# Where to form two small weight sums: GpSimd in the first GEMM of block 1, or VectorE in its second GEMM

## Chip, core and metric

The kernel runs on one core of one Trainium2 chip. The metric is the time of one execution on the device in microseconds. The engines named below are PE (TensorE; its weight loads are listed apart as PEld), DVE (VectorE), ACT (ScalarE), POOL (GpSimd) and SP (SyncE, which here only issues transfers).

## What is computed

A retention layer feeds a feed-forward block. All data are fp32.

```python
# retention, per batch and head: gamma_h = 1 - 2**(-5-h), scale = 1/sqrt(64)
state = gamma * state + outer(k[t], v[t])
y[t]  = scale * q[t] @ state
x = y.transpose(0, 2, 1, 3).reshape(3072, 512)      # 4 batches x 768 tokens, 8 heads x 64
# feed-forward
h = x @ w_in                                        # 512 -> 2048, the first GEMM
g = where(h > 0, h, exp(min(h, 0)) - 1)             # ELU
out = g @ w_out                                     # 2048 -> 512, the second GEMM
```

## The kernel before

The 3072 tokens are cut into six blocks of 512, called 0 to 5. Both GEMMs save products in the manner of Strassen: a product of two matrices, each cut in 2x2 quarters, is made of seven smaller products M1 to M7 of sums of quarters, and the results are put together from their sums. Block 0 has a plain first GEMM and Strassen once in the second. Block 1 has Strassen once in the first GEMM and twice (a Strassen inside each of the seven products) in the second. Blocks 2 to 5 have it twice in the second GEMM, and in the first for two of the seven products, M2 and M3.

The Strassen inside M2 and M3 of the first GEMM needs four sums of quarters of their weights, for each of the two. These eight "small" sums are the subject here. They are the same for all blocks, so they are made once, sent to DRAM (`scratch3`) and fetched again in each of blocks 2 to 5 through a ring of 11 weight tiles (`wq`, pool `ring`), which `fetch_small` fills: each product that has used a tile asks for the next fetch. The fetches, the loads of new tokens and the stores all go through SP's one queue, in the order of the program.

The order on every engine is the order in which the program writes the instructions (`manual_schedule`). Generators are used to interleave: `first(n)` is one of four steps (n = 0 to 3) of block 1's first GEMM, `second_twice(1, ...)` its second GEMM, and each `yield` is a place where other work can be put.

The parts that matter here, with their lines in the kernel before:

- `first(n)` (L728) goes through `strassen` (L698). Product 7 starts a new accumulation in the single PSUM bank `pd`. The same bank was last read by `plus(pd, u2)` (L695) for product 4 of the step before. So the first weight load of product 7 waits for that VectorE addition. In step n the products are written as 1, 2, then the rest of the step before (3, 4, and the ELU of its last quarter), then 6, 7, 5. The ELU of a quarter is two ScalarE operations (L477, L478) and one VectorE operation (L481).
- `sides[n]` are VectorE sums for later steps, put between the products of step n: `combine_w_in` (L674) and the remaining part of `combine_w_out` (L647), whose results are sent by `send_small` (L641).
- `combine_small(j)` (L810) makes the four small sums of M2 (j = 2) or M3 (j = 3) on GpSimd, in a tile `wi` of the pool `stage`. It is called at the end of step n = 0 for M2 and of step n = 2 for M3, followed by `send_small`.
- `scale_v(m)` (L275, L281) multiplies the v of a loaded chunk of 128 tokens by a table; from chunk 2 on it runs on GpSimd. `load(8)` to `load(11)` are written one in each step n, and the four `scale_v(8)` to `scale_v(11)` after the loop, behind `combine_small` on GpSimd.
- The pools `stage` and `t4` are then closed (L1302), and `ring` and `tpool` take their memory.
- `second_twice(1, ...)` (L933): for each of seven outer products in the order 1, 2, 6, 7, 5, 3, 4, `inner(j)` (L967) runs seven inner products of four 128x128 matmuls. PE sees them as 1, 2, then 3 and 4 of the outer product before, then 6, 7, 5. Inner product 4 adds to the PSUM bank `pd` after VectorE has read it in `add(res[:, 1, 1], pd, ...)` (L983), so its first weight load waits for that addition. `input_parts` (L941) makes four VectorE sums (`ts`, L827) for the next outer product.
- The loop at L1318 counts outer products in `step` and puts the retention of block 2 (`retention_step`) at the places in `VISITS`. `outputs_step` starts with two small copies (`seen`, L378) that wait for PE.
- `xt_` (L266) holds the activations x of block 1. They are read last by the first GEMM of block 1. The memory is written again in block 2 by `combine_x_parts` (L454).

Of the kernel before, what the change touches and what calls it, by code (L numbers as in the profile page):

```python
# [9 lines left out]
FP32 = mybir.dt.float32  # L10
# [8 lines left out]
def kernel(  # L19
# [32 lines left out]
    nc = tc.nc  # L52
    PSUM = bass.MemoryType.PSUM
    P = nc.NUM_PARTITIONS
# [29 lines left out]
    stage = early.enter_context(tc.tile_pool(name="stage", bufs=3))  # L84
# [14 lines left out]
    def load(m, parts=1):  # L99

        if m >= NCHUNK:
            return
        t = ldpool.tile([P, 2048], FP32, name="chunk", tag="chunk")
        raw[m] = (
            t[:, 0:1024].rearrange("p (a h c) -> p a h c", a=2, c=C),
            t[:, 1024:2048].rearrange("p (a h d) -> p a h d", a=2, d=D),
        )
        for part in range(parts):
            c = slice(part * 2048 // parts, (part + 1) * 2048 // parts)
            nc.sync.dma_start(t[:, c], qkv[m, :, c])  # L110

    def hold(t, other):

        if other is not None:
            nc.gpsimd.tensor_copy(t[0:1, 0:1], other[0:1, 0:1])
# [6 lines left out]
    w_a, w_b, w_s = ([x[:, n] for n in range(NQ)] for x in (w_a_, w_b_, w_s_))  # L122
# [100 lines left out]
    for h in range(H):  # L223
# [11 lines left out]
        out=causal, in_=causal, compare_op=ALU.is_gt, fill=1.0, base=0, pattern=[[-1, P]], channel_multiplier=1  # L235
# [30 lines left out]
    xt_ = const.tile([P, 4, 2, TH], FP32, name="xt")  # L266
# [45 lines left out]
    def scores(tb, pp):  # L312

        sc = [ps_r.tile([P, 2, HP, D], FP32, name="sc", tag="r") for _ in range(2)]
        for x in range(2):
            score_products(sc, tb, pp, x)
        for a in range(2):
            nc.vector.tensor_tensor(
                out=raw[tb * CPB + 2 * pp + a][0][:, 1].rearrange("p h c -> p (h c)").rearrange("p (n t) -> p n t", t=D),
                in0=sc[a].rearrange("p x h t -> p (x h) t"),  # L320
                in1=cmask.unsqueeze(1).to_broadcast([P, 2 * HP, D]), op=ALU.mult,
            )
# [29 lines left out]
    def states(tb, pp):  # L352

        kvs = [ps_r.tile([P, 2, HP, D], FP32, name="kv", tag="r") for _ in range(2)]
        for x in range(2):
            state_products(kvs, tb, pp, x, range(2))
        for x in range(2):
            for sub in range(2):
                state_sum(kvs, tb, pp, x, sub)
# [4 lines left out]
    def outputs(tb, pp):  # L364

        y = [ps_r.tile([P, 2 * 2, 2, D], FP32, name="y", tag="r") for _ in range(2)]
        for x in range(2):
            for j in range(4):
                pt = raw[tb * CPB + 2 * pp + j // 2][0][:, 1].rearrange("p h c -> p (h c)")
                within(tb, pp, x, j, y, lambda p: pt[:, (x * HP + p) * D :][:, 0:D])  # L370
        for other in range(2):
            if not other:
                yield
            else:

                for sub in range(2):
                    seen = epool.tile([P, 8], FP32, name="seen", tag="seen")
                    nc.vector.tensor_copy(seen.rearrange("p (j x) -> p j x", x=2), y[sub][:, :, :, 0])  # L378
                yield
            for x in range(2):  # L380
                across(tb, pp, x, other, y)
        i = chunks[tb * CPB + 2 * pp][1]
        for sub in range(2):
            nc.vector.tensor_tensor(
                out=place_of(x_of(tb)[:, :, 2 * pp * C : 2 * (pp + 1) * C])[:, :, :, sub, :], in0=y[sub],
                in1=place_of(powers[:, :, i * C : (i + 2) * C])[:, :, :, sub, :], op=ALU.mult,
            )
# [26 lines left out]
    def outputs_of_first():  # L414

        y = [bank(x).rearrange("p a (b x d) -> p (a b) x d", b=2, x=2) for x in "bd"]
        for x in range(2):
            for j in range(4):
                pt = raw[x][0][:, 1].rearrange("p h c -> p (h c)")
                within(0, 0, x, j, y, lambda p: pt[:, ((j // 2) * HP + p) * D :][:, 0:D])  # L420
            yield
            across(0, 0, x, 0, y)
            for sub in range(2):
                if not fresh(0, 2 * x + sub):
                    seen = epool.tile([P, 8], FP32, name="seen", tag="seen")
                    nc.vector.tensor_copy(seen[:, 0:4], y[sub][:, :, x, 0])
            if x:
                yield
            across(0, 0, x, 1, y)
            if x:  # L430
                yield
            for sub in range(2):
                nc.vector.tensor_tensor(
                    out=place_of(xb[:, :, 0 : 2 * C])[:, :, x, sub, :], in0=y[sub][:, :, x],
                    in1=place_of(powers[:, :, 0 : 2 * C])[:, :, x, sub, :], op=ALU.mult,
                )
            if not x:
                yield

    def outputs_step(tb, step):  # L440

        if step == 0:
            held["y"] = [outputs(tb, pp) for pp in range(2)]
        if step < 2:
            next(held["y"][step])
            next(held["y"][step])
        else:
            for g in held["y"]:
                next(g, None)
# [18 lines left out]
    def flush():  # L468
        while later:
            later.pop(0)()  # L470
# [109 lines left out]
    def small_of_pieces(at):  # L580

        sources = [
            (decoded[2 * NQ + n].rearrange("p r (d c) -> p (r d) c", d=2)[:, 1:4], sums[n])
            for n in (2 * at, 2 * at + 1)
        ]
        return combine_w_out(at, *sources)
# [54 lines left out]
    def send_small():  # L641
        while to_send:
            nc.sync.dma_start(*to_send.pop(0))
# [163 lines left out]

    W_IN = {2: w_a_[:, :, :, 1], 3: w_s_[:, :, 2]}

    def combine_small(j, behind=None):  # L810

        t = stage.tile([P, 4, 4, P], FP32, name="wi", tag="stage")
        hold(t.rearrange("p k f d -> p (k f d)"), behind)
        a11, a12, a21, a22 = (W_IN[j][:, 2 * r : 2 * r + 2, :, c, :] for r in range(2) for c in range(2))
        s1, s2, s3, s4 = (t[:, k].rearrange("p (n f) c -> p n f c", f=2) for k in range(4))
        tt = lambda o, x, y, op: nc.gpsimd.tensor_tensor(out=o, in0=x, in1=y, op=op)
        tt(s1, a21, a22, ALU.add)
        tt(s2, s1, a11, ALU.subtract)
        tt(s3, a11, a21, ALU.subtract)
        tt(s4, a12, s2, ALU.subtract)  # L820
        to_send.append((scratch3[j - 1], t.rearrange("p k f d -> p (k f d)")))

    xs = {}

# [295 lines left out]
    y = outputs_of_first()  # L1120
# [39 lines left out]
    y = outputs(0, 1)  # L1160
# [24 lines left out]
    for n, _ in enumerate(inner):  # L1185
# [19 lines left out]
        elif n == 12:  # L1205
            smalls = small_of_pieces(0)
# [12 lines left out]
    for n in second_of_first():  # L1219
# [6 lines left out]
        elif n == 1:  # L1226
            smalls = small_of_pieces(1)
# [33 lines left out]
    def retention_step(tb, step):  # L1261
        if tb >= NTB:
            return
        if step == 0:
            scores(tb, 0)
            scores(tb, 1)
        elif step == 1:
            states(tb, 0)
            states(tb, 1)
        elif step < 5:  # L1270
            outputs_step(tb, step - 2)
# [4 lines left out]
    sides = [  # L1276
        itertools.chain(combine_w_in(1), last), itertools.chain(combine_w_in(2), combine_w_in(3)), iter(()), iter(()),
    ]
    smalls = [2], [], [3], []
    for n in range(NQ):  # L1280
        load(2 * CPB + n)
        cur = first(n)
        for at in range(3):
            next(cur)

        for _ in tail:
            pass
        for s in cur:
            next(sides[n], None)
            next(sides[n], None)  # L1290
            if s == "gap":
                break
        for _ in sides[n]:
            pass
        tail = cur
        for j in smalls[n]:
            combine_small(j, w_s[1].rearrange("p s a b c -> p (s a b c)") if j == 2 else None)
        send_small()
    for m in range(2 * CPB, 3 * CPB):
        scale_v(m)  # L1300
# [14 lines left out]
        pass  # L1315
    flush()
    step, VISITS = 0, [(0, "end"), (2, "middle"), (3, "first"), (4, "end"), (5, "end")]
    for s in sec:  # L1318
        if s == "first":
            step += 1  # L1320
        at = (step, s if s in ("first", "middle") else "end")
        if at in VISITS:
            retention_step(2, VISITS.index(at))
        if s == ORDER2[-1]:
            break
    tail = sec
# [2 lines left out]
    for tb in range(2, NTB):  # L1329
        more = tb + 1 < NTB  # L1330
        qa, qd, u2, end = {}, {}, {}, None
# [43 lines left out]
        for n in range(NQ):  # L1375
# [17 lines left out]
            end = first_end(n, "C12", qa[n])  # L1393
            other = first_end(n, "C22", qa[n], m7)
            if n < 3:
# [5 lines left out]
                end = first_end(n, "C21", qd[n], u2[n])  # L1401
# [10 lines left out]
        end = first_end(3, "C21", qd[3], u2[3])  # L1412
# [64 lines left out]
```

## Time and profile before

| quantity | value |
|---|---|
| time, median of 3 runs | 636.76 us (635.6 to 637.08) |
| span of the profiled run | 634.4 us |
| PE busy | 626.7 us (99%) |
| DVE busy | 481.7 us (76%) |
| ACT busy | 252.9 us (40%) |
| POOL busy | 40.6 us (6%), 40 instructions |
| mean DMA rate | 216 GB/s |
| PE's share of the chain that ended last | 94% |

The chain that ended last is the list of work that set the end, followed back from the last instruction. Where an engine has 94% of it, only time in which that engine stands still can be won by moving other work. The rest of the reading is therefore a search for places where PE, or its weight load PEld, waits.

In this trace block 1's first GEMM lies at about 135 to 182 us and its second GEMM at about 182 to 240 us, counted from the start of the span.

### The profile page before, as it was taken

To read this page: it belongs to the slowest core of one execution; us is meant where nothing else is said; L and a number is where in the kernel's file an instruction comes from. 1 tells how busy PE (TensorE), PEld (TensorE's weight loads), DVE (VectorE), ACT (ScalarE), POOL (GpSimd) and SP (SyncE) were. 2 spreads that over 40 slices of the span, in tenths; PEclk is the share of its full clock that TensorE was granted. 3 is DMA by queue.
4 is the path that set the end of the run, shared out by engine and by line. 5 is a ranking of instruction groups with operands and counts; after the bars stand their busy time and mean duration, and the time that the engine had idled before them with its cause. 6 is when DMAs were issued, how large, how long until landed. Compare 5 with 4: busy or idle time off the path is not lost.

```text
span 634.4 us, 16149 instructions
## 1 busy us (share of the span) xinstructions
PE 626.7 (99%) x6680; PEld 560.7 (88%) x6680; DVE 481.7 (76%) x870; ACT 252.9 (40%) x472; POOL 40.6 (6%) x40
## 2 busy tenths in 40 slices
PE   8999999999999999999999999999999999999998
PEld 5764568888899999889999989999988999988997
DVE  5779979978879685589676598867489878558975
ACT  6599635014551113554112556111465311366311
POOL 1111000003600000200000100000110000000000
PEclk9999999999999999999999999999999999999999
DMA  8698867687477778504889701789820697700794
GB/s 336 264 390 307 269 205 222 189 248 258 176 239 228 242 254 272 239 2 135 277 267 312 290 4 55 258 283 286 302 100 4 218 299 236 238 24 2 231 309 158
DMA packets 75897, 136.85 MB, mean 216 GB/s; under 512 B 6320, under 2 KB 31792, under 8 KB 70704
## 3 DMA queue, kind: packets, MB, share of 16 engines
q1 hardware_dynamic: 75824, 135.82, 64.2%
q8 instruction: 53, 0.87, 0.5%
q14 instruction: 20, 0.16, 0.1%
HBM read 114.56 MB, written 21.23 MB: 214 GB/s over the span
## 4 chain that ended last, share of the span: by engine, by line
PE 94%; DVE 4%; issue 1%; ACT 0%; DVEq 0%
PE pa L953 20%; PE pa L911 10%; PE pd L953 10%; PE pb L953 5%; PE pa L865 5%; PE pb L911 4%; PE pa L521 3%; PE qa L911 3%; PE x L611 3%; PE pa L740 2%; PE pd L865 2%; PE qd L911 2%; PE pd L911 2%; PE pa L611 2%; PE y L394 2%; PE kv L338 2%
## 5 line engine op out<-in xcount | busy, mean ns | idle before, releaser
L961 ACT COPY ms<-pa 128x128 f32<-128x128 f32 x104 | 27.6, 265 | 147.1 <-PE pa L953 143.7
L953 PE MATMUL pa<-ts,wq 128*128 128x128 f32 x560 | 74.2, 275 | 0.0
L953 PE MATMUL pd<-ts,wq 128*128 128x128 f32 x552 | 73.6, 276 | 0.1
L953 PEld LDWEIGHTS pa<-ts,wq 128*128 128x128 f32 x560 | 68.5, 192 | 0.4
L953 PEld LDWEIGHTS pd<-ts,wq 128*128 128x128 f32 x552 | 67.1, 192 | 0.9 <-DVE res L965 0.5
L953 PE MATMUL pa<-gC,wq 128*128 128x128 f32 x480 | 64.6, 278 | 0.0
L478 ACT ACTIVATE r<-r 128x512 f32<-128x512 f32 x96 | 60.5, 631 | 3.0
L953 PEld LDWEIGHTS pa<-gC,wq 128*128 128x128 f32 x480 | 59.0, 192 | 1.3
L477 ACT ACTIVATE r<-gC 128x512 f32<-128x512 f32 x64 | 39.9, 624 | 32.0 <-DVE gC L919 32.0
L965 DVE TENSOR_TENSOR res<-pd,ms 128x128 f32<-128x128 f32 x68 | 19.4, 286 | 39.6 <-PE pd L953 38.4
L281 POOL TENSOR_TENSOR chunk<-chunk,vf 128x512 f32<-128x512 f32 x22 | 26.3, 1199 | 318.4 <-DMA chunk<-in_qkv_dram 153.5
L481 DVE SCALAR_TENSOR_TENSOR gC<-r,gC 128x512 f32<-128x512 f32 x64 | 44.3, 724 | 0.7 <-ACT r L478 0.7
L827 DVE TENSOR_TENSOR ts<-gC,ts 128x512 f32<-128x512 f32 x60 | 41.3, 688 | 1.0
L827 DVE TENSOR_TENSOR ts<-gC 128x512 f32<-128x512 f32 x60 | 40.9, 682 | 0.0
L953 PE MATMUL pb<-gC,wq 128*128 128x128 f32 x240 | 31.7, 275 | 0.0
L986 ACT COPY res<-pa 128x128 f32<-128x128 f32 x34 | 9.0, 265 | 55.1 <-PE pa L953 55.1
L953 PEld LDWEIGHTS pb<-gC,wq 128*128 128x128 f32 x240 | 29.2, 192 | 0.0
L690 ACT COPY m<-pa 128x512 f32<-128x512 f32 x24 | 13.9, 581 | 30.1 <-PE pa L911 14.2
L919 DVE TENSOR_TENSOR gC<-qa,gC 128x512 f32<-128x512 f32 x8 | 5.5, 692 | 25.1 <-PE qa L911 18.3
L911 PE MATMUL pa<-xt,w_s 128*128 128x256 f32 x96 | 23.0, 382 | 0.0
L911 PE MATMUL pa<-xt,w_b 128*128 128x256 f32 x96 | 23.0, 382 | 0.0
L965 DVE TENSOR_TENSOR res<-res 128x512 f32<-128x512 f32 (+1 forms) x31 | 20.6, 666 | 3.0 <-DVE res L965 0.5
(256 smaller groups left out, 1258.4 us busy)
## 6 DMA issues: line engine op xcount, KB each, us to landing
wq<-scratch_dram SPq DMA_DIRECT2D x277, 256.0 KB, 4.2
chunk<-in_qkv_dram SPq DMA_DIRECT2D x23, 1024.0 KB, 8.3
wraw<-in_w_dram SPq DMA_DIRECT2D x15, 1024.0 KB, 6.1
out_dram<-res SPq DMA_DIRECT2D x14, 256.0 KB, 3.8
scratch_dram<-gT SPq DMA_DIRECT2D x12, 256.0 KB, 4.2
scratch_dram<-m SPq DMA_DIRECT2D x12, 192.0 KB, 5.6
scratch_dram<-so SPq DMA_DIRECT2D x4, 512.0 KB, 4.8
scratch_dram<-wi SPq DMA_DIRECT2D x2, 1024.0 KB, 5.1
```

The source lines that it names most:

```text
L281: eng.tensor_tensor(out=kv[:, 1], in0=kv[:, 1], in1=vf[:, i].unsqueeze(2).to_broadcast([C, H, D]), op=ALU.mult)
L477: nc.scalar.activation(e, h, AF.Relu, scale=-1.0)
L478: nc.scalar.activation(e, e, AF.Exp, scale=-1.0)
L481: nc.vector.scalar_tensor_tensor(g, e, -1.0, h, ALU.add, ALU.max)
L521: nc.tensor.matmul(hp, lhsT=w[n][:, fi, j // 2, j % 2, :], rhs=xb[:, j, :], start=(j == 0), stop=(j == 3))
L611: nc.tensor.matmul(X[j][:, d, :], lhsT=w[j][:, d * P : d * P + P], rhs=x[j], start=(n == 0 and d == 0), stop=at_end, skip_group_check=True,)
L827: sub = lambda o, x, y: nc.vector.tensor_tensor(out=o, in0=x, in1=y, op=ALU.subtract)
L865: nc.tensor.matmul(ps[:, f, :], lhsT=lhs[f], rhs=xs[j][k], start=(begin and f == 0), stop=True, skip_group_check=True,)
L911: nc.tensor.matmul(ps[:, fi, :], lhsT=w[:, fi, j2, :], rhs=x[:, j2, :], start=(j in (1, 7) and fi == 0 and j2 == 0), stop=(j2 == 1), skip_ ...
L953: nc.tensor.matmul(ps, lhsT=w[:, f, :], rhs=ts[j][k][:, f, :], start=(begin and f == 0), stop=(f == 3), skip_group_check=True,)
L961: nc.scalar.copy(m, ps)
L965: nc.vector.tensor_tensor(out=o, in0=x, in1=y, op=ALU.add)
```

## The change

The eight sums are made by VectorE, in block 1's second GEMM, and in the memory of x (`xt_`), which is free there. `combine_small` becomes a generator of two parts with two sums each. The parts are put in four places of the second GEMM, and the two transfers to DRAM in two. GpSimd keeps only the scaling of v. The purpose is to take GpSimd's work out of the first GEMM and to put the sums where VectorE has idle time.

```diff
-    def combine_small(j, behind=None):
-        t = stage.tile([P, 4, 4, P], FP32, name="wi", tag="stage")
-        hold(t.rearrange("p k f d -> p (k f d)"), behind)
+    def combine_small(j):
+        t = xt_.rearrange("p j a (b c) -> p j (a b) c", c=P)
...
-        tt = lambda o, x, y, op: nc.gpsimd.tensor_tensor(out=o, in0=x, in1=y, op=op)
+        tt = lambda o, x, y, op: nc.vector.tensor_tensor(out=o, in0=x, in1=y, op=op)
         tt(s1, a21, a22, ALU.add)
         tt(s2, s1, a11, ALU.subtract)
+        yield
         tt(s3, a11, a21, ALU.subtract)
         tt(s4, a12, s2, ALU.subtract)
         to_send.append((scratch3[j - 1], t.rearrange("p k f d -> p (k f d)")))
+        yield
...
-    smalls = [2], [], [3], []
     for n in range(NQ):
...
-        for j in smalls[n]:
-            combine_small(j, w_s[1].rearrange("p s a b c -> p (s a b c)") if j == 2 else None)
         send_small()
...
+    smalls = itertools.chain(combine_small(2), combine_small(3))
+    SUMS = [(3, "first"), (3, "middle"), (4, "end"), (5, "first")]
     for s in sec:
...
         if at in VISITS:
             retention_step(2, VISITS.index(at))
+        if at in SUMS:
+            next(smalls)
+        if at in ((3, "end"), (5, "middle")):
+            send_small()
```

In the counting of `step`, 3 is outer product 7, 4 is outer product 5 and 5 is outer product 3.

## Prediction

> **What bounds the kernel now.** I read the page first: PE is 99% busy and has 94% of the chain that ended last, so a change can only win where PE stands still. The waits of PE's weight load show where:
>
> ```profile
> PEld pd L740 <- DVE h L695: 2.0, 2, 1.1
> ...
> PEld pd L953 <- DVE res L965: 0.5, 2, 0.3
> ```
>
> Each row gives the total, the number of waits and the longest. The first is in block 1's first GEMM: product 7 wants bank `pd`, and VectorE has not yet read it out. The second is the same kind of wait in a second GEMM. The timeline of PEld shows both cases of the first row:
>
> ```profile
> 150.72 1.70 PEld L740 LDWEIGHTS pa<-xb,w_s 128*128 128x128 f32 x8
> 153.55 1.59 PEld L740 LDWEIGHTS pd<-xb,w_s 128*128 128x128 f32 x8 [1.13 <-DVE h L695]
> ...
> 163.88 1.70 PEld L740 LDWEIGHTS pa<-xb,w_s 128*128 128x128 f32 x8
> 166.42 1.59 PEld L740 LDWEIGHTS pd<-xb,w_s 128*128 128x128 f32 x8 [0.84 <-DVE h L695]
> ```
>
> Unstalled groups follow each other every 1.73 us (x8 at 171.56, 173.29, 175.01). So the two groups were due at 152.44 and 165.60. Followed to the third group after, 156.97 and 169.84, the losses are 156.97 - 150.72 - 3 x 1.725 = 1.07 us and 169.84 - 163.88 - 5.175 = 0.78 us. Together **1.85 us**, the most the change can win here (0.29%). From 170 to 240 us the chain is PE without a gap.
>
> Why was VectorE late? Its timeline beside GpSimd's:
>
> ```profile
> 146.14 1.63 DVE L647 TENSOR_TENSOR wi<-w_s 128x384 f32<-128x384 f32 x1
> 147.81 1.51 DVE L647 TENSOR_TENSOR wi<-wi,w_s 128x384 f32<-128x384 f32 x1
> 149.24 0.54 DVE L647 TENSOR_TENSOR wi<-w_s 128x384 f32<-128x384 f32 x1
> ```
>
> ```profile
> 145.63 1.73 POOL L816 TENSOR_TENSOR wi<-w_a 128x512 f32<-128x512 f32 x1
> 147.31 1.58 POOL L816 TENSOR_TENSOR wi<-w_a,wi 128x512 f32<-128x512 f32 x1
> ```
>
> The same VectorE operation takes 0.54 us alone and 1.5 to 1.6 us beside a small sum on GpSimd. The second stall has the M3 sums beside it (POOL from 162.26 to 168.1).
>
> [...] an addition that reads PSUM is not stretched (`h` at 165.69: 0.68 us beside POOL). The scaling of a chunk does the same to VectorE as a small sum, which decides this prediction:
>
> ```profile
> 262.51 1.37 DVE L481 SCALAR_TENSOR_TENSOR gC<-r,gC 128x512 f32<-128x512 f32 x2
> ...
> 265.25 2.13 DVE L481 SCALAR_TENSOR_TENSOR gC<-r,gC 128x512 f32<-128x512 f32 x2
> ```
>
> ```profile
> 264.67 1.57 POOL L281 TENSOR_TENSOR chunk<-chunk,vf 128x512 f32<-128x512 f32 x1 [1.94 <-DMA chunk<-in_qkv_dram]
> ```
>
> A pair that another place runs in 1.28 us (284.22) takes 2.13 us: **0.85 us per scaling**. ([...] scalings alone take 1.04 us.) [...] the trace has 680 to 690 ns, and starts 0.60 us apart (0.71 when one needs the one before). [...]
>
> **The change, part by part.** Times are those of the trace before.
>
> 1. *GpSimd's eight sums and the one-element copy go.* Step n = 1: VectorE's four L647 operations start at about 146.1 and follow at 0.46 us (as 149.24 to 149.70; 0.57 for the dependent one), so `h` of product 2 starts at 148.03 instead of 150.17. Then come two ScalarE operations of 0.66 us and an L481, up to about 150.7, and `h` of product 4, which cannot start before its matmuls end (149.21 + 1.89 = 151.10). It ends at 151.83; the weight load is due at 152.44. **First stall gone: +1.07 us**, with 0.6 us to spare.
>
> 2. *Step n = 2, if nothing else happened.* From that `h` to the next `h` of product 2 VectorE is busy without a gap: 152.82 to 162.10 before, 9.28 us. So 151.14 + 9.28 = 160.42. From there to the weight load it takes 0.69 (h) + 1.36 (two ScalarE operations) + 0.60 (L481) + 0.69 + 0.05 = 3.39 us: 163.81. It is due at 165.60 - 1.07 = 164.53. Slack 0.72 us, second stall gone as well.
>
> 3. *But the chunk scalings move forward.* They stood behind the small sums on GpSimd (168.09 to 172 and 175.53, where VectorE had slack). Now each runs when its transfer lands. On SP, chunks 9 to 11 follow the eight L643 sends with no small sum between, so they go out at about 148.5 to 150 instead of 151.4, 152.7 and 168.5. Before, 3.93 MB of sends and loads took 148.5 to 160.9. Now the last sends (0.6 MB) and three chunks (3.15 MB) are in line from 147.5; at 410 GB/s, the rate from 156.5 to 158.5, chunks land at about 153, 155.5 and 158. All three fall into the gapless stretch of step 2 (151.7 to 161), whose operations have two SBUF inputs but for one. 3 x 0.85 = 2.55 us. (Chunk 8 lands near 143, when VectorE idles.) Lateness at product 7: 2.55 - 0.72 = **1.83 us**, in place of the 0.78. Bounds for one scaling: 0.62 us (the L481 at 175.82 took 1.30 instead of 0.68) and 1.04 us (the whole of it). Lateness 1.14 to 2.40.
>
> Sum of the first GEMM: 1.85 - 1.83 = +0.02 us won, bounds -0.55 and +0.71. With two hits +0.87, with one 1.72.
>
> 4. *VectorE gains eight sums of 0.60 to 0.71 us, 5.1 us together*, in the second GEMM, in four pairs of 1.2 to 1.3 us. VectorE idles there (3.1 us of 5 from 215 to 220), but what counts is the addition behind them that frees `pd`:
>
> ```profile
> 217.72 0.97 PEld L953 LDWEIGHTS pd<-ts,wq 128*128 128x128 f32 x8
> ```
>
> ```profile
> 212.47 0.24 DVE L378 COPY seen<-y 128x8 f32<-128x8 f32 x2 [0.47 <-PE y L409]
> ...
> 215.65 0.29 DVE L965 TENSOR_TENSOR res<-pd,ms 128x128 f32<-128x128 f32 x1 [0.41 <-ACT ms L961]
> ```
>
> After `seen` come now two sums, four `ts`, two sums and then this `res`. From 212.63: 1.32 + 2.52 + 1.20 = 217.67, end 217.96, load at about 218.0 against 217.72: **0.28 us lost**. The `ts` are wanted at 218.6 and later and are ready. The first pair for M3 stands at 224.42 before a wait of 0.72 us and another of 1.43 and is hidden. The last pair follows 228.78: 229.39 + 1.20 + 2.52 = 233.11 for `res`, end 233.40, load 233.44 against 233.27: **0.17 us lost**. Behind it, four L384 end at 235.8, and the load that reads `xb` is due at 236.84; the sums for block 2 end at 238.4, wanted at 242.2. Hidden. Total 0.45 us, bounds 0 (if sums run 5% quicker) and 0.9 (double).
>
> 5. *Transfers.* The send of M2 waits for its sums until 217.8, and three ring fetches behind it on SP, due at 216.24, 217.1 and 218.0, leave at 218.2 and after. A tile freed at 216.24 is wanted 11 products on, 226.62. At 4.4 us plus 2.6 us behind the 1 MB send (410 GB/s) it is there at 225.2: hidden by 1.4 us. M3 writes the same memory at 224.7, when the send (5.1 us) is done at 222.9. The send of M3 leaves at 230.7; the first fetch of it, due at about 232.6, must wait until 236 and holds what is behind it for 4 us. Its tile is wanted at 247.6. Chunk 12's load moves by some 2 us and is wanted after 260. The next writer of `xt`, at 241.67, comes later too. Nothing there.
>
> 6. *Memory.* `wi` of the small sums no longer delays the ring, whose first fetches went out at 173.0 for use at 182; earlier fetches win nothing. Hidden.
>
> **Sum**: +0.02 - 0.45 = 0.43 us slower, 637.2; the spread of the three runs before is 1.5 us. I take **637.1**, no measurable change: one stall goes, the other grows by as much.
>
> **Rivals.**
>
> - *Faster*: scalings miss the chain (later landing, or VectorE goes first), and both stalls vanish: 636.76 - 1.85 + 0.45 = 635.4. For it: the whole loss sits beside the small sums, and a window of some us decides. Against: three chunks would have to land outside 10 us in which the queue has nothing else to bring.
> - *Slower*: the late fetches starve the ring. Against a slowest landing of 7.6 us before, with 2.6 us for the send, the tile comes at 228.4 and PE waits 1.8 us: 637.2 + 1.8 = 639.0. With dearer scalings alone (1.04 us each) it is 637.8. Against: 1.4 us of slack at usual landings.
>
> **How the numbers follow.** Forecast 0.60, faster 0.16, slower 0.24. The forecast's case spans its bounds, 636.1 to 638.2. The range reaches from the faster case, 635.3, to 638.7, between the forecast's upper bound and the slower case, and leaves out some 0.15. The limit of 0.2% is 1.27 us: the faster case is just past it; the slower case beyond.
>
> **What would show it.** Right: in the PEld timeline no wait before the `pd` group of step n = 1, a longer one (about 1.8 us) before that of n = 2, three L281 on POOL between 151 and 162, and VectorE rows of 1.3 to 1.7 us beside them; waits of PEld on `res` near 218 and 233. Wrong: no PEld wait on `h` at all (then faster), waits of PE on the transfer of `wq` near 226 (slower), or L281 outside that window.

## The result, and the profile after

The kernel after takes 638.88 us (median of 20 runs, 636.91 to 645.02). The kernel before, timed beside it on the same chip, takes 636.53 us (20 runs, 634.71 to 640.36). The ratio is 1.0044, with a 95% interval of 1.0028 to 1.0060. **The change makes the kernel slower, by 1.8 to 3.8 us.** The forecast was 637.1 us and no measurable change.

In the kernel after, the line numbers below the diff are higher by one or two. L815 are the eight sums, L828 makes `ts`, L954 is the matmul of an inner product and L966 is the addition that ends in `res`.

The first view is the page of the kernel after, its row of busy times (us, share of the span, instructions):

```profile
PE 626.6 (99%) x6680; PEld 561.0 (88%) x6680; DVE 481.7 (76%) x878; ACT 253.0 (40%) x472; POOL 28.8 (5%) x31
```

GpSimd went from 40.6 to 28.8 us, as meant. VectorE is busy for as long as before (481.7 us) with 878 instructions instead of 870. From 135 to 182 us, with fewer operations lengthened beside GpSimd, it is busy for 33.26 us instead of 37.95; from 182 to 240 us, where the eight sums now are, for 49.86 instead of 45.84. So the change did what it set out to do, and the time went elsewhere. The waits of PE's weight load (in all, how many, the longest) say where:

```profile
PEld pa L954 <- issue: 1.7, 1, 1.7
...
PEld pd L954 <- DVE res L966: 1.3, 3, 0.9
PEld pd L740 <- DVE h L695: 1.0, 1, 1.0
```

The wait for `h` is 1.0 us instead of 2.0, one place instead of two. The wait for `res` is 1.3 instead of 0.5. And a wait of 1.7 us is new whose releaser is "issue": nothing that the profile shows ended it. The timeline of PEld, first GEMM:

```profile
149.99 1.70 PEld L740 LDWEIGHTS pa<-xb,w_s 128*128 128x128 f32 x8
151.72 1.70 PEld L740 LDWEIGHTS pd<-xb,w_s 128*128 128x128 f32 x8
...
162.08 1.70 PEld L740 LDWEIGHTS pa<-xb,w_s 128*128 128x128 f32 x8
164.78 1.59 PEld L740 LDWEIGHTS pd<-xb,w_s 128*128 128x128 f32 x8 [1.00 <-DVE h L695]
```

The first stall is gone; the second is still there (due at 163.80, 0.98 us late). Counted to the third group after, which starts at 168.19 and was due at 162.08 + 3 x 1.725 = 167.26, 0.93 us is lost here. Before, 1.85 us was lost in all. **The first GEMM won 0.92 us.** The second GEMM, same view:

```profile
216.38 0.97 PEld L954 LDWEIGHTS pd<-ts,wq 128*128 128x128 f32 x8 [0.22 <-DVE res L966]
...
223.49 0.19 PEld L954 LDWEIGHTS pa<-gC,wq 128*128 128x128 f32 x1
225.34 0.86 PEld L954 LDWEIGHTS pa<-gC,wq 128*128 128x128 f32 x7 [1.66 <-issue]
...
233.85 0.97 PEld L954 LDWEIGHTS pd<-ts,wq 128*128 128x128 f32 x8
...
236.64 0.97 PEld L954 LDWEIGHTS pd<-ts,wq 128*128 128x128 f32 x8 [0.92 <-DVE res L966]
```

Groups of eight follow each other every 0.89 to 0.90 us when nothing is in the way. From the starts, 0.30 us is lost before 216.38, 0.19 before 233.85 (after 232.77) and 1.0 before 236.64 (two groups after 233.85, so due at 235.64). The wait of 1.66 us is in the *middle* of a group: one load ran, and the other seven of product 3 of outer product 5 came later, although they read the same tiles. In sum 0.30 + 0.19 + 1.0 + 1.66 - 0.92 = 2.2 us are lost in this profiled run, inside the interval of the timed runs. (The two spans, 634.4 and 635.9, differ by less, since the profiled run of after was 0.73 us ahead already from 83 us on, before anything that the change touches.)

Two readings had to be explained: the wait of 1.0 us for `res`, and the one without a releaser. For the first, VectorE's timeline suffices:

```profile
229.78 0.68 DVE L815 TENSOR_TENSOR xt<-w_s 128x512 f32<-128x512 f32 x1
230.38 0.68 DVE L815 TENSOR_TENSOR xt<-w_s,xt 128x512 f32<-128x512 f32 x1
...
233.52 0.28 DVE L966 TENSOR_TENSOR res<-pd,ms 128x128 f32<-128x128 f32 x1
233.72 2.47 DVE L384 TENSOR_TENSOR xb<-y,etab 128x512 f32<-128x512 f32 x4
236.11 0.28 DVE L966 TENSOR_TENSOR res<-pb,ms 128x128 f32<-128x128 f32 x1
236.31 0.28 DVE L966 TENSOR_TENSOR res<-pd,ms 128x128 f32<-128x128 f32 x1
```

The last two sums push everything behind them by 1.2 us: the first `res`, four L384, and then a second `res<-pd` at 236.31, whose end at 236.59 releases the load at 236.64. That load opens product 7, which takes bank `pd` anew. In the kernel before the same addition ended at 234.99 and the load started on time at 235.05: a slack of 0.06 us, in a place where the timeline shows no wait at all. The two lines of before, VectorE and PEld:

```profile
234.71 0.28 DVE L965 TENSOR_TENSOR res<-pd,ms 128x128 f32<-128x128 f32 x1
```

```profile
235.05 0.97 PEld L953 LDWEIGHTS pd<-ts,wq 128*128 128x128 f32 x8
```

### The profile page after: what moved, and what is told of

Same layout as the page of the kernel before. It is cut to its first block, busy times and chain, and to the rows that moved or that the text cites. A ratio compares the mean times of both kernels' runs of the same rounds, so it can differ in the third digit from the quotient of the medians.

```text
span 635.9 us, 16146 instructions
## 1 busy us (share of the span) xinstructions
PE 626.6 (99%) x6680; PEld 561.0 (88%) x6680; DVE 481.7 (76%) x878; ACT 253.0 (40%) x472; POOL 28.8 (5%) x31
## 4 chain that ended last, share of the span: by engine, by line
PE 94%; DVE 3%; DMA 1%; issue 1%; ACT 0%; SPq 0%; DVEq 0%
PE pa L954 19%; PE pa L912 10%; PE pd L954 10%; PE pb L954 5%; PE pa L866 5%; PE pb L912 4%; PE pa L521 3%; PE qa L912 3%; PE x L611 3%; PE pa L740 3%; PE pd L866 2%; PE qd L912 2%; PE pa L611 2%; PE pd L912 2%; PE y L394 2%; PE sc L307 2%
## 5 line engine op out<-in xcount | busy, mean ns | idle before, releaser
L954 PE MATMUL pd<-ts,wq 128*128 128x128 f32 x552 | 73.8, 277 | 0.8 <-DVE res L966 0.7
L954 PE MATMUL pa<-ts,wq 128*128 128x128 f32 x560 | 74.2, 276 | 0.0
L954 PEld LDWEIGHTS pa<-ts,wq 128*128 128x128 f32 x560 | 68.5, 192 | 0.4
L954 PEld LDWEIGHTS pd<-ts,wq 128*128 128x128 f32 x552 | 67.1, 192 | 1.9 <-DVE res L966 1.3
L954 PE MATMUL pa<-gC,wq 128*128 128x128 f32 x480 | 64.9, 278 | 1.5 <-issue 1.5
L954 PEld LDWEIGHTS pa<-gC,wq 128*128 128x128 f32 x480 | 59.1, 192 | 2.9 <-issue 1.7
L966 DVE TENSOR_TENSOR res<-pd,ms 128x128 f32<-128x128 f32 x68 | 19.4, 286 | 40.1 <-PE pd L954 39.3
L481 DVE SCALAR_TENSOR_TENSOR gC<-r,gC 128x512 f32<-128x512 f32 x64 | 42.8, 700 | 0.7 <-ACT r L478 0.7
L828 DVE TENSOR_TENSOR ts<-gC,ts 128x512 f32<-128x512 f32 x60 | 41.3, 688 | 1.0
L828 DVE TENSOR_TENSOR ts<-gC 128x512 f32<-128x512 f32 x60 | 40.9, 682 | 0.0
L954 PE MATMUL pb<-gC,wq 128*128 128x128 f32 x240 | 31.7, 275 | 0.0
L954 PEld LDWEIGHTS pb<-gC,wq 128*128 128x128 f32 x240 | 29.2, 192 | 0.0
L912 PE MATMUL pa<-xb,w_a 128*128 128x256 f32 x96 | 22.7, 379 | 0.0
```

The costliest lines, as they stand in the source:

```text
L481: nc.vector.scalar_tensor_tensor(g, e, -1.0, h, ALU.add, ALU.max)
L828: sub = lambda o, x, y: nc.vector.tensor_tensor(out=o, in0=x, in1=y, op=ALU.subtract)
L912: nc.tensor.matmul(ps[:, fi, :], lhsT=w[:, fi, j2, :], rhs=x[:, j2, :], start=(j in (1, 7) and fi == 0 and j2 == 0), stop=(j2 == 1), skip_ ...
L954: nc.tensor.matmul(ps, lhsT=w[:, f, :], rhs=ts[j][k][:, f, :], start=(begin and f == 0), stop=(f == 3), skip_group_check=True,)
L966: nc.vector.tensor_tensor(out=o, in0=x, in1=y, op=ALU.add)
```

## The experiments

Each ratio is a kernel's time over that of the kernel before, with a 95% interval. It is estimated from the runs of both, and differs a little from the quotient of the two medians. The profile of a kernel is one run of it.

For the 1.66 us the theory was formed after the result. **PE ran out of instructions.** The profile lists a DMA queue "q8 instruction" with 53 packets of 16 KB; 6680 loads and 6680 matmuls are 252 for each packet, and 257 with the semaphore instructions on PE (13614 in the trace of before). By these numbers the packets are taken to be PE's instructions, one block of about 256 in each. The DMA view of half a microsecond (number of packets, MB, share) finds the packet between 222.0 and 222.5 us in the kernel before, and between 223.0 and 223.5 us in the kernel after (in this order):

```profile
q1 hardware_dynamic: 95, 0.17, 92.5%
q8 instruction: 1, 0.02, 11.7%
```

```profile
q1 hardware_dynamic: 103, 0.18, 101.3%
q8 instruction: 1, 0.02, 11.7%
```

In narrower windows it begins at 222.3 before and 223.05 after. PE goes on 2.3 us after that, at 225.34. Before, the group that the edge falls in ran in one piece:

```profile
224.83 0.97 PEld L953 LDWEIGHTS pa<-gC,wq 128*128 128x128 f32 x8
```

PE needed the instruction behind the edge (the end of one block and the start of the next) only with the second of these loads, at 224.94. With the 2.3 us of the kernel after, the block was there at 222.3 + 2.3 = 224.6, in time by about 0.3 us; this is an estimate from the two profiles. The rival was that PE waits for a fetched weight, behind the send in the ring, and the profile fails to name it.

### 1. Parts of the change alone

**The eight sums alone**, on VectorE in the four places of the change, into `xt`, beside the GpSimd ones, not sent:

```diff
+    def extra_small(j):          # as combine_small after, without to_send
...
+        if at in SUMS:           # (3, first), (3, middle), (4, end), (5, first)
+            next(extra)
```

> The kernel before, and in its second GEMM of block 1 the eight VectorE sums of the change as well, into the memory of x, at the same four places; GpSimd's sums stay and are the ones sent. Both theories expect PE's weight load to wait for the additions res near the places seen after the change (0.3, 0.2 and 1.0 us, 1.5 us together). Theory VectorE (all of the loss comes from VectorE being late for bank pd): the change lost 2.35 us and its first GEMM won 0.92, so this kernel must lose about 3.3 us against before (ratio 1.005). Theory transfers (the sends add a loss of their own, in which PE waits for nothing that the profile names): it loses 1.5 us (ratio 1.0024) and shows no such wait.

637.75 us against 636.45, ratio 1.0025 (1.0009 to 1.0041). The PEld timeline has the waits for `res` of the kernel after, to 0.01 us, and no wait without a releaser near 225 us:

```profile
217.70 0.97 PEld L966 LDWEIGHTS pd<-ts,wq 128*128 128x128 f32 x8 [0.22 <-DVE res L978]
236.22 0.97 PEld L966 LDWEIGHTS pd<-ts,wq 128*128 128x128 f32 x8 [0.93 <-DVE res L978]
```

(L966 and L978 are here the load and `res`.) So the sums as placed cost about 1.5 us, and nothing else is needed for that.

**The two sends alone**, waiting for nothing:

```diff
+        if at in ((3, "end"), (5, "middle")):
+            nc.sync.dma_start(scratch3[3 + step // 5], xt_.rearrange("p j a t -> p (j a t)"))
```

> The kernel before, and in its second GEMM of block 1 two more transfers of 1 MB from the memory of x to two unused parts of scratch3, at the places of the two sends of the change, waiting for nothing; no sums are added. Theory VectorE: nothing is behind a VectorE operation, so 0 us, ratio 1.000. Theory transfers: 1.8 us slower (ratio 1.003), times further apart than before, in the profile stalls of PE named issue or DMA between 215 and 240 us.

637.07 us, ratio 1.0017 (1.0004 to 1.0029), a smaller loss than the 1.003 expected of the transfers. The wait without a releaser is there, after the same one load of the same product, with no operation added on PE, VectorE, ScalarE or GpSimd:

```profile
225.04 0.86 PEld L953 LDWEIGHTS pa<-gC,wq 128*128 128x128 f32 x7 [0.57 <-issue]
```

The transfers are enough to bring it, then, and the prediction had costed them at nothing. (This profile has another wait of the kind, 1.50 us at 304.25, far behind the sends; see the last section.)

### 2. Parts of the change undone

**Scalings held**: one copy on GpSimd, which waits for a result of step n = 2, stands ahead of the four `scale_v`.

```diff
+    late = const.tile([P, 1], FP32, name="late")
+    nc.gpsimd.tensor_copy(late[0:1, 0:1], gq["T3"][0:1, 5, 0:1])
     for m in range(2 * CPB, 3 * CPB):
         scale_v(m)
```

> The changed kernel, with one GpSimd copy of one element ahead of the four scalings of v; it waits for a VectorE result of step n = 2 (about 165 us), so that the scalings come when VectorE has idle time. Both theories: the one remaining wait of the first GEMM (0.98 us before product 7 of step 2) goes, so 0.9 us less than the changed kernel: 637.9 or ratio 1.0029 to before if the rest stays as it is. If instead VectorE's lateness there has another cause than the scalings, nothing changes.

636.95 us, ratio 1.0012 (1.0001 to 1.0023). The scalings run from 177.8 us on, and the wait for `h` before `pd` is gone altogether:

```profile
162.58 1.70 PEld L740 LDWEIGHTS pa<-xb,w_s 128*128 128x128 f32 x8
164.31 1.70 PEld L740 LDWEIGHTS pd<-xb,w_s 128*128 128x128 f32 x8
```

That it was the scalings that left the second stall standing is shown by this. The time fell by more than that wait: 1.0029 was expected, outside the interval. The waits for `res` and the one without a releaser (1.12 us) remain.

**Sums moved** to where VectorE is idle and no release of `pd` is near:

```diff
-    SUMS = [(3, "first"), (3, "middle"), (4, "end"), (5, "first")]
+    SUMS = [(3, "first"), (3, "end"), (4, "end"), (4, "end")]
...
-        if at in SUMS:
+        for _ in range(SUMS.count(at)):
             next(smalls)
```

> The changed kernel, with the second pair of sums of M2 moved behind the addition that frees bank pd, and the second pair of M3 moved forward beside the first, into 2.6 us of VectorE idle time; the sends stay at their places. The waits of PE's weight load on res (0.3, 0.2 and 1.0 us) should go. Theory VectorE: only the win of the first GEMM is left, 0.9 us faster than before, ratio 0.9986. Theory transfers: 1.5 us less than the changed kernel, still 0.9 us slower than before, ratio 1.0014, with the unnamed wait of PE.

636.45 us, ratio 0.9998 (0.9984 to 1.0013). Of the waits for `res` 0.2 us in all is left. The waits for `h` (1.1 us) and without a releaser (1.38 us) stay. The time lies between the 0.9986 and the 1.0014 of the two theories; it is the wait that speaks for the transfers.

**Both**:

> The kernel after with both repairs: the sums at later visits (M2 in the third outer product's first and last places, M3 in the fourth's last), so that nothing waits for res, and the chunk scalings held on GpSimd until the third step of the first GEMM is over. Theory (three separate costs that add: the first GEMM's wait before pd, the waits for res, the wait for instructions): 0.9 us under the kernel with the sums moved alone, ratio 0.9985, no wait for h before pd, none over 0.2 us for res, and the wait without a releaser near 225 still there at 0.5 to 1.7 us. Rival (the wait before pd is made up for later, or the scalings, made later, hold back the third chunk group): no better than the sums moved alone, ratio 0.9998.

635.80 us against 636.50, ratio 0.9994 (0.9978 to 1.0010); expected was 0.9985, inside the interval, but so is the rival's 0.9998. In the waits of PEld the three costs are seen to be separate: none for `h` before `pd` in the first GEMM, 0.2 us for `res`, and 0.57 us without a releaser. In the times they are not: the two repairs took 0.0032 and 0.0046 off the ratio of the kernel after, each alone, and 0.0050 together. The intervals are too wide to say more.

### 3. Is it the fetch of instructions?

**A shifted stream.** Eight more matmuls on blanks, in the idle time before the first chunk has landed. The page counts 16 loads and 16 matmuls more, so every later instruction of PE lies 32 further on, and nothing else changes:

```diff
-    for n in range(28):
+    for n in range(36):
```

> The kernel after, with eight more idle-time warm-up matmuls of 64 x 64 before the first chunk has landed (36 instead of 28): the same work everywhere else, but every later TensorE instruction lies 32 instructions further on in the stream. Theory A (the wait without a releaser inside product 3 of outer product 5 is TensorE out of instructions, at the edge of a fetched block): the wait leaves that product and appears two products of 16 loads and matmuls earlier, in product 1 of outer product 3, at about 221 to 223 us, again after one load and matmul; no wait without a releaser stays at product 3. Theory B (it is a wait for a fetched weight or for the ring, which the profile fails to name): it stays in product 3 of outer product 5, 0.5 to 1.7 us. Time: as after, ratio 1.003 to 1.006, or up to 0.002 less under A when the fetch meets less traffic.

```profile
223.74 0.30 PEld L954 LDWEIGHTS pa<-gC,wq 128*128 128x128 f32 x2
227.53 0.75 PEld L954 LDWEIGHTS pa<-gC,wq 128*128 128x128 f32 x6 [3.50 <-issue]
```

The wait has left product 3 of outer product 5 and stands two groups earlier, in product 1 of outer product 3, after two loads: 15 loads and their matmuls earlier, for 16 added. A wait for a weight or for a tile would have stayed with its product. **It is the edge of a block of instructions.** Counting PE's instructions in the traces (loads, matmuls and semaphores) says the same: 4801 or 4802 of them precede the wait in each of the ten kernels that have it (table below), the shifted one included. Waits of this kind elsewhere, near 67 and 303 us, stand 3072 instructions before that place and 1792 behind it, 12 and 7 times 256, to within one instruction. The wait was also longer, 3.5 us, and the kernel slower: 640.89 us, ratio 1.0075 (1.0051 to 1.0099), more than I had expected. PE reaches the edge two groups, 1.8 us, sooner in its work, while the fetch begins no sooner, at 225.04; and the wait for `h` in the first GEMM was 1.7 us in this profile, where it is 1.0 in the kernel after.

**The same in all kernels.** For each profile, the start of the packet (that of the window of about 0.1 us in which it was found, so up to 0.14 us early) against the start of the last load before the edge (where no wait shows the edge, the first load of that group; for the shifted stream the second, 0.11 us after the first). The lead is the time from the one to the other:

| kernel | fetch begins | last load before the edge | lead | wait |
|---|---|---|---|---|
| before | 222.3 | 224.83 | 2.5 | none |
| sums alone | 222.0 | 224.81 | 2.8 | none |
| VectorE in the first GEMM (below) | 221.8 | 224.57 | 2.8 | none |
| late send (below) | 221.1 | 223.98 | 2.9 | none |
| first send alone (below) | 224.8 | 226.66 | 1.9 | 0.28 |
| both sends alone | 222.6 | 224.28 | 1.7 | 0.57 |
| sums moved and scalings held | 221.6 | 223.12 | 1.5 | 0.57 |
| M2 sent in halves (below) | 221.5 | 222.91 | 1.4 | 0.84 |
| first send doubled (below) | 223.1 | 224.43 | 1.4 | 0.84 |
| early send (below) | 223.7 | 225.01 | 1.3 | 0.84 |
| scalings held | 222.1 | 223.20 | 1.1 | 1.12 |
| sums moved | 223.4 | 224.18 | 0.8 | 1.38 |
| after | 223.05 | 223.49 | 0.4 | 1.66 |
| shifted stream | 225.04 | 223.85 | -1.2 | 3.50 |

In all ten with a wait, lead and wait add up to 2.05 to 2.3 us; the four without a wait have a lead of 2.5 us or more. So what the wait costs is settled by when the fetch begins. The ten are also the kernels in which 1 MB or more is sent from x's memory some 5 to 12 us ahead of the fetch; none of the four has such a send there. The last section shows such waits that came without a send near them, so one profile alone would prove little; ten against none is hard to put down to chance.

### 4. What delays the fetch

**The first send alone**, to see whether it or the second one matters:

```diff
+        if at == (3, "end"):
+            nc.sync.dma_start(scratch3[3], xt_.rearrange("p j a t -> p (j a t)"))
```

> The kernel before, with only the first of the two extra 1 MB sends out of x's memory in the third outer product (scratch3[3], read by nobody); GpSimd still makes M2 and M3, and no operation is added on an engine. Theory A (TensorE's next block of instructions is fetched through the DMA engines, at about 222 to 223 us, and stands behind the first send and the fetches of small weights): the wait without a releaser in the group of product 3 of outer product 5, near 224.5 to 225, is there as with both sends, 0.4 to 1.1 us, and the ratio is 1.0007 to 1.0017, the larger part of what the two sends cost (1.0017). Theory B (the second send, near 231 us, is what costs): no such wait near 225, ratio 1.000.

The wait is at its place after one load, 0.28 us, shorter than I had expected. The time, 636.88 us against 636.50, ratio 1.0000 (0.9983 to 1.0017), can't be told from no change. The second send isn't needed for the wait.

**Two MB at that place** (the line above twice, to two parts of the scratch memory), and **M2 in halves**: in the kernel with both repairs, 512 KB at (3, "end") and 512 KB at (4, "first"), with M3 in two halves at its one place.

> The kernel before with two extra 1 MB sends out of x's memory back to back at the place of the change's first send (third outer product's end; they write parts of the scratch memory that nobody reads); nothing added on an engine, GpSimd still makes M2 and M3. Theory A (the fetch of TensorE's instructions stands in the backlog that the send makes, so the wait grows with the bytes sent there): the wait without a releaser in product 3 of outer product 5 grows from 0.28 us with one send by roughly the time that one more MB takes at the 0.30 MB per us that these 10 us moved, some 3 us, to 2 to 4 us in all; ratio 1.003 to 1.007; or fetched weights come late too and TensorE waits for wq. Theory B (the wait there is chance or belongs to the send's existence, not its size): it stays at 0.3 to 0.6 us, ratio 1.000 to 1.0015.

> The kernel after with both repairs (sums moved to later visits, scalings held) and M2 sent in two halves of 512 KB, at the third outer product's end and the fourth's first place, instead of 1 MB at once; M3 in two halves at its one place. Theory A: the backlog in front of TensorE's instruction fetch at 222 us is about halved, so the wait without a releaser near 224 us falls from 0.57 to 0 to 0.3 us; ratio 0.997 to 0.999, under the 0.9994 of the kernel with one send. Theory B (the backlog is that of the fetches of small weights, not of the send): the wait stays at 0.5 us or more, ratio 0.999 to 1.000.

Both figures that theory A gave for the wait missed. With twice the bytes it is 0.84 us where 2 to 4 was expected, ratio 1.0007 (0.9993 to 1.0020). With M2 in halves it is 0.84 us as well, not less, ratio 0.9985 (0.9966 to 1.0004). With single sends of 1 MB the wait was 0.28 to 1.66 us, so 2 MB brought no more than these, and spreading the send over 3.6 us did not remove it.

**An earlier and a later send**: one MB at (3, "first"), issued at 211.46, and at (4, "end"), issued at 221.11, the same moment at which the fetch begins.

> The kernel before with one extra 1 MB send as before, two visits earlier (third outer product's first place instead of its end), some 4 us earlier; nothing else. In the kernels so far the wait in product 3 of outer product 5 is 2.05 to 2.27 us less the lead of the fetch of instructions over TensorE's arrival (lead 2.5 to 2.8 us without a send, 0.4 to 1.9 with one). Theory A (what delays the fetch is the transfer traffic of the 6 us before it, and the send has to stand in those): lead back over 2.2 us, no wait there; ratio 0.9995 to 1.001. Theory B (any extra MB in this stage delays the fetches behind it for the whole stage): lead under 2.1 us and a wait of 0.2 to 0.8 us.

> The same send, at the fourth outer product's end, after TensorE's fetch near 222 us has begun. Theory A: lead over 2.4 us as without a send, no wait in product 3 of outer product 5; if the next fetch, near 229 us, has little lead, a wait without a releaser shows some microseconds later instead. Theory B (the wait there has nothing to do with the place of the send): a wait of 0.2 to 0.8 us stays there.

```profile
226.05 0.86 PEld L953 LDWEIGHTS pa<-gC,wq 128*128 128x128 f32 x7 [0.84 <-issue]
```

```profile
223.98 0.97 PEld L953 LDWEIGHTS pa<-gC,wq 128*128 128x128 f32 x8
```

The first fence is the early send, with the wait after one load of the group; the second the late one, the same group in one piece. With the early send the fetch 12 us behind it began at 223.7 and PE waited; with the late one, on its way only after the fetch had begun at 221.1, PE did not. The times, 636.33 and 637.11 against 636.32, ratios 1.0006 (0.9993 to 1.0019) and 1.0007 (0.9991 to 1.0023), settle nothing. So in these profiles a MB ahead of this fetch was enough to make it late, whether issued 5 us ahead (216.28 against 221.6, sums moved and scalings held) or 12. How busy the DMA engines are does not tell which kernel waits: their share from 216 to 222 us is 0.82 before and 0.91 after, but 0.82 as well with the sums moved (wait 1.38 us) and with the shifted stream (3.50 us). Where in the DMA engines the packet stands, and why its delay was 0.6 us in one kernel and 2 us in another, is **open**: the trace does not say which engine a packet ran on.

### 5. A version that is faster than both

If GpSimd's sums harm VectorE beside them, and sends in the second GEMM harm PE's fetches, the sums belong on VectorE in the first GEMM. M2's four go to a gap of step n = 0 (in the staging memory), M3's four to step n = 2 (in the memory of `so`, not in use then), the sends stay where they were, and the scalings are held.

```diff
-        tt = lambda o, x, y, op: nc.gpsimd.tensor_tensor(out=o, in0=x, in1=y, op=op)
+        tt = lambda o, x, y, op: nc.vector.tensor_tensor(out=o, in0=x, in1=y, op=op)   # a yield after each but the last
...
-        itertools.chain(combine_w_in(1), last), itertools.chain(combine_w_in(2), combine_w_in(3)), iter(()), iter(()),
+        itertools.chain(combine_w_in(1), combine_small(2), last), itertools.chain(combine_w_in(2), combine_w_in(3)),
+        combine_small(3), iter(()),
...
-        for s in cur:
-            next(sides[n], None)
-            next(sides[n], None)
+        for i, s in enumerate(cur):
+            for _ in range(5 if (n, i) == (0, 1) else 2):
+                next(sides[n], None)
...
```

> The kernel before, with VectorE making M2 and M3 in the first GEMM itself, in its own idle time (M2 in the first step, after the sums of the first GEMM's weights, in the staging memory; M3 in the third step, in so's memory), the two sends where they were, and the chunk scalings held until the third step is over. GpSimd does nothing beside VectorE's operations there. Theory (both waits before pd in the first GEMM, 1.07 and 0.80 us, come from GpSimd's operations slowing VectorE's; sends in the second GEMM are what is to be avoided): both waits gone, no new wait in the second GEMM, 1.5 to 1.9 us under the kernel before, ratio 0.997 to 0.9976. Rival (VectorE's eight sums, 0.6 us each, delay h as long as GpSimd's did): a wait for h stays at one of the two places, ratio 0.999 to 1.001.

634.57 us (7 runs) against 636.50, **ratio 0.9964 (0.9949 to 0.9979)**: 1.9 us gained between the medians, about what was lost in the first GEMM before (1.85 us). M2's sums stand where VectorE had been idle or stretched, each at its own length, and the `pd` groups of both steps start on time, 1.73 us behind the group ahead (153.89 after 152.16; 165.98 after 164.25). VectorE (first and last of M2's sums), then PEld in step n = 1:

```profile
143.95 0.68 DVE L818 TENSOR_TENSOR wi<-w_a 128x512 f32<-128x512 f32 x1
...
145.88 0.68 DVE L818 TENSOR_TENSOR wi<-w_a,wi 128x512 f32<-128x512 f32 x1
```

```profile
152.16 1.70 PEld L740 LDWEIGHTS pa<-xb,w_s 128*128 128x128 f32 x8
153.89 1.70 PEld L740 LDWEIGHTS pd<-xb,w_s 128*128 128x128 f32 x8
```

## Why the prediction was wrong, step by step

Steps 4 and 5 failed. Steps 1 to 3 were right in their mechanism; the size in step 3 was off.

**Step 1** (first stall gone, +1.07) was right: the `pd` group of step n = 1 starts at 151.72, on time.

**Step 2** (0.72 us of slack in step n = 2 without scalings) agrees with the run that held them: no wait there.

**Step 3** (three scalings land in the gapless stretch) was right, with a term too large. They ran where foretold, and VectorE beside them:

```profile
154.53 1.57 POOL L281 TENSOR_TENSOR chunk<-chunk,vf 128x512 f32<-128x512 f32 x1 [11.03 <-DVE w_b L674]
157.03 1.11 POOL L281 TENSOR_TENSOR chunk<-chunk,vf 128x512 f32<-128x512 f32 x1 [0.94 <-DMA chunk<-in_qkv_dram]
159.53 1.40 POOL L281 TENSOR_TENSOR chunk<-chunk,vf 128x512 f32<-128x512 f32 x1 [1.38 <-DMA chunk<-in_qkv_dram]
```

```profile
155.23 1.42 DVE L674 TENSOR_TENSOR w_s<-w_a,w_s 128x512 f32<-128x512 f32 x1
...
157.17 0.68 DVE L695 TENSOR_TENSOR h<-pd,m 128x512 f32<-128x512 f32 x1
157.77 0.93 DVE L481 SCALAR_TENSOR_TENSOR gC<-r,h 128x512 f32<-128x512 f32 x1
...
160.06 1.42 DVE L674 TENSOR_TENSOR w_s<-w_a,w_s 128x512 f32<-128x512 f32 x1
```

Three scalings of 0.85 us were to cost 2.55. They cost 0.73 + 0.25 + 0.73 = 1.7 us. The middle one lay for most of its length beside `h`, which reads PSUM and is not stretched (0.68 us); the prediction had said so of `h`, and hadn't applied it. Lateness at product 7 was 0.98 us, not 1.83. So the first GEMM won 0.92 us, not 0.02: outside the bounds of -0.55 to +0.71, on the good side, and close to the +0.87 that the prediction gave for two hits.

**Step 4** (eight sums, 0.45 us) had its two terms right, 0.30 and 0.19 us for 0.28 and 0.17. Its sentence "Hidden" for what stands behind the four L384 failed: it checked the load that reads `xb` and the sums for block 2, and not the two additions between them, the second of which frees `pd` for product 7. It had 0.06 us of slack. That is 1.0 us, the missing term; the step's upper bound of 0.9 was for dearer sums, not for a forgotten release.

**Step 5** (transfers: "Nothing there") failed. The step looked for waits on fetched weights, and there are none, as it said. It did not count the fetch of PE's own instructions among the transfers: 1.66 us in the profile of after. In the kernel before that fetch was in time by about 0.3 us, as estimated above. The wait that it did foresee is there: on SP the first fetch of M3 waits for 3.4 us, until the send of M3 has landed at 236.99, where the step had 236 and 4 us.

**Step 6** holds; no wait points to the memory.

With the measured terms in its own sum: +0.92 - 1.49 - 1.66 = -2.23, so 2.2 us slower, where it had 0.43. The rival "slower" gave nearly the right time, 639.0, for the wrong reason: no tile of the ring came late. What the prediction said would show it wrong, waits on the transfer of `wq` near 226, was not seen; the wait 0.7 us away had another cause.

## What to carry to other kernels

When work is put on an engine that has idle time, list every operation behind it up to the next real wait of that engine, and for each that frees a buffer, how long before the waiting instruction it ended: a slack of 0.06 us looks like no wait at all. Price a transfer that is added to a busy stage by what else is fetched in that stage, the instructions of an engine without any pause included: here PE waited 0.28 to 1.66 us with single sends of 1 MB ahead of such a fetch. What gave it away was a wait of "issue" in the middle of a uniform group, which moved by 15 loads and their matmuls when 16 were added far ahead of it. And when work is taken off one engine, ask what stood behind it in that engine's queue, since that will now run earlier: three scalings of v, which had stood behind the small sums until 168 us and later, ran at 154.5 to 160.9 us in the kernel after.

## What the runs showed of the hardware

- PE's fetch of instructions was mostly in time, but not always. In the kernel before, at the 53 places that lie a multiple of 256 instructions from the edge at 224.94 (to within three), PE waits without a releaser for 0.33 us at most. In the kernels in which the fetch near 222 us was late, PE resumed 2.2 to 2.5 us after the 16 KB packet began, and had stood for 0.28 to 3.5 us.
- The same wait turns up where no edit reaches, so it may be a part of the spread of the runs. At one edge, near 303 us, five of the 14 profiles have it, of 0.40 to 1.94 us, among them that of the eight sums alone (0.68 us), where no transfer was added. In the kernel with the early send one of 1.46 us stands at 67.04, before the send, 2.3 us after a packet at 64.76. The longest of those near 303 us, in the kernel with the sums moved and the scalings held, 2.4 us after a packet at 301.1:

```profile
303.53 0.20 PEld L409 LDWEIGHTS y<-chunk 64*64 64x64 f32 x6 [1.94 <-issue]
```

- Moving the stream of one engine by 32 instructions, with no work of weight added, went with a ratio of 1.0075 (1.0051 to 1.0099) where the kernel after has 1.0044 (1.0028 to 1.0060), each against before; the intervals overlap, so the times alone don't show a cost of the shift. In the profiles the wait at the edge is 3.50 us instead of 1.66. Differences of this size between two kernels can thus come in part from where their blocks of instructions end.
